# Values in 32-column tiles turned by VectorE, with new planner costs, in a routing-attention and MLP-mixer kernel

## The chip, the core and the metric

The kernel runs on one core of one Trainium2 chip. The metric is the device time of one execution in microseconds (us). Three executions of the kernel before took 811.82 us in the median (810.64 to 812.14).

A core has five engines with queues of their own, each worked off in order: TensorE (matmuls, "PE" in the profile, with its weight loads as "PEld"), VectorE ("DVE"), ScalarE ("ACT"), GpSimd ("POOL") and SyncE ("SP"). SP issues nearly all DMAs here; a few stand in ScalarE's queue. The on-chip memory is one array, `arena`; matmul results land in eight banks of PSUM, `ps`.

## The reference, cut to what is computed

```python
# q, k, v: (4, 8, 768, 64); centroids: (8, 16, 64), all f32
c_n = centroids / (norm(centroids) + 1e-06)                # q_n and k_n likewise
q_assign = argmax(einsum('bhsd,hcd->bhsc', q_n, c_n), -1)  # k_assign likewise
mask = q_assign[:, :, :, None] == k_assign[:, :, None, :]
scores = where(mask, (1 / sqrt(64)) * q @ k^T, -1e9)
attn = softmax(scores) @ v                                 # per batch and head
x = attn.transpose(0, 2, 1, 3).reshape(4, 768, 512)
h = relu(x^T @ w_tok1) @ w_tok2                            # (512, 768) by (768, 256) by (256, 768)
u = x + h^T
out = u + relu(u @ w_ch1) @ w_ch2                          # (768, 512) by (512, 1536) by (1536, 512)
```

The weights of the mixer come as 8-byte words, and the kernel rebuilds f32 values from their two halves with integer work on VectorE (`weight_round`).

## The kernel before, in words

**Recording and planning.** The kernel doesn't emit instructions directly. Helpers (`mm`, `copy`, `halves`, `tt`, `vec`, `dma`, `transpose`) record operations in a `Program`, each with the engines that may run it, a cost in us, and the parts of memory that it reads and writes. `Program.run` plans: matmuls keep the order in which they were recorded; on every other engine, an operation is chosen among those that are ready in the plan, by its due time. The plan is made with `COST`, `LAT` and the costs written at the calls, and the instructions are then emitted in the planned order. Since a helper records everything, nearly all matmuls have line L829, all two-input adds L868, ScalarE's and VectorE's plain copies L848 and L850, copies of 16-bit halves L858, DMA issues L888 and DMA transposes L893.

**Attention.** There are 4 batches x 8 heads; two heads form a pair, so 16 pairs `m`, one after the other. The 768 tokens of a pair are 6 tiles of 128, or two halves of 384. Per pair TensorE does, in this order:

- `scores`: 12 chunks (two halves `u` of the queries by six key tiles `i`). In each chunk, two f32 matmuls of 64 rows, one for each head, and two bf16 matmuls that add the mask out of one-hot cluster codes `M`. ScalarE takes the exp of 768 columns of each chunk (L1122) out of one of three pairs of PSUM banks.
- `values`: 24 matmuls of 64 columns by 384, two heads beside each other, into banks 6 and 7; the result has head dimension by token. ScalarE copies it to `avs`.
- `route` for pair `m + 2`: four matmuls of 32 columns by 384 give the cluster scores. On VectorE: a transpose of 32x32 blocks out of PSUM (L1044), a maximum (L1045), a comparison, a transpose back (L1049). On ScalarE: the one-hot codes `rb` with a count of hits (L1053). `rb` then goes through DRAM into `M`; for pair 0 through eight small DMAs inside `arena`.
- `sums`: VectorE adds up the exps over key tiles (three adds for each half, two of 1536 and one of 768 columns), four matmuls with a matrix of ones give the softmax denominators, which are copied to `denS`.
- `finish_x`: six transposes of `avs` and three of `denS` on TensorE; on VectorE the reciprocal, and two multiplications out of PSUM that write `x`.

For pairs 0 to 2 the queries and keys are turned by TensorE (`turn_qk`). From pair 3 on `dma_turn_qk` does it: ScalarE takes the 16-bit halves apart (four copies of 768 columns), two DMA transposes turn them, and ScalarE joins them in two copies of 1536 columns. Meanwhile VectorE prepares the mixer's weights in 31 pieces of up to 512 columns, together with the sums that the seven-product scheme below needs, and stores them in DRAM (`wdt`, `wd1`, `wd2`).

**Mixer.** All four products of the mixer are done as seven half-size products in place of eight (`token1`, `token2`, `product`), with sums and differences on VectorE and GpSimd. `channel1` and `channel2` run over two groups of two batches. In them GpSimd does differences of operands (`tsum`) and sums of products (`combine`) on 384 or on 3 x 384 columns, VectorE drains PSUM with adds (L868) and does the other sums, ScalarE the relu (L875). Out of the same weights ScalarE computes range sums (L1759), and `check` (L1771 to L1804) compares counts at the end, in the middle of the last group's work; a general path stands behind a flag and isn't taken here.

**Before the first scores.** The centroids are loaded and normed on VectorE, turned on TensorE and copied into `cbd`; pair 0 is loaded by two queues (keys by SP, queries by ScalarE's), turned, routed; pair 1 is turned while the codes of pair 0 are made; three chunks of scores without mask are done ahead, then `route(1)`, then the masks.

## Time and profile before

| What | us |
|---|---|
| Profiled execution, its own time | 812.03 |
| its span | 810.2 |
| Median of three executions | 811.82 |
| Start of the first masked scores | 19.13 |
| First weight load of pair 1's scores | 41.26 |
| First matmul of the mixer | 345.03 |
| Last matmul | 804.8 |

How to read the lines: times are in us from the start of the span unless marked ns. A group line gives line, engine, operation, output and input shapes (partitions x elements) and count, then busy time and the mean ns of one, then the idle time of the engine just before them and what ended it. A timeline line gives start, duration, engine, line and operation; equal neighbours are merged with their count, and the bracket tells how long the engine was idle before, and who released it. A line of the windows view gives a stretch, its length, the busy time and count of each engine, the granted TensorE clock, the share of busy DMA engines, and GB/s. An f32 matmul is recorded as two, each with its own weight load. The ends of matmuls are modelled, so the spacing of weight loads tells more about TensorE's pace than its busy time does.

### The profile page before, as it was taken

The numbers are of one execution on the slowest core, as the hardware profiler recorded it, in microseconds if no ns is written. First come the engines' busy times: TensorE is split into PE (matmuls) and PEld (weight loads), VectorE is DVE, ScalarE is ACT, GpSimd is POOL, SyncE is SP. The second block draws the span as 40 slices with busy tenths as digits, with TensorE's granted clock in tenths as the row PEclk, the third lists the DMA queues.
The fourth block names the chain that finished last, engine by engine and source line by source line (L and its number), as shares of the span: only waits on it lengthen the run. The fifth ranks groups of instructions, "written<-read, shape, count | busy, mean of one in ns | idle before, by whom it ended". The sixth has DMA issues, their size and how long they took to land.

```text
span 810.2 us, 10859 instructions
## 1 busy us (share of the span) xinstructions
PE 791.3 (98%) x3743; PEld 429.2 (53%) x3743; DVE 678.1 (84%) x873; ACT 473.0 (58%) x612; POOL 178.8 (22%) x124
## 2 busy tenths in 40 slices
PE   5999999999999999999999999999999999999997
PEld 3444445554444445444555555555555555555554
DVE  3789999999999999998898867699975686789984
ACT  3688888888888875699913236433464504400424
POOL 1000000000000000000345398500196379620000
PEclk9999999999999999999999999999999999999999
DMA  5777778879888984369739765556899833333766
GB/s 123 213 181 179 179 195 207 211 181 226 204 210 182 226 236 115 82 132 222 146 85 260 202 199 177 184 176 202 239 252 239 223 109 107 97 96 99 160 156 167
DMA packets 265120, 143.49 MB, mean 177 GB/s; under 512 B 184289, under 2 KB 260961, under 8 KB 265057
## 3 DMA queue, kind: packets, MB, share of 16 engines
q1 hardware_dynamic: 262560, 141.88, 68.7%
q10 hardware_dynamic: 2496, 0.84, 0.4%
q8 instruction: 32, 0.52, 0.3%
q14 instruction: 32, 0.25, 0.1%
HBM read 91.95 MB, written 28.61 MB: 149 GB/s over the span
## 4 chain that ended last, share of the span: by engine, by line
PE 95%; DVE 1%; issue 1%; DMA 0%; ACT 0%; SPq 0%; ACTq 0%
PE ps L829 95%; DVE arena L868 0%; DVE arena L850 0%; DMA arena<-arena 0%; ACT arena L1122 0%; ACT arena L848 0%; SPq L888 0%; DVE arena L1244 0%; DVE arena L1045 0%; DVE arena L1044 0%; ACT arena L1053 0%; DVE arena L1790 0%; ACTq L848 0%
## 5 line engine op out<-in xcount | busy, mean ns | idle before, releaser
L829 PE MATMUL ps<-arena 128*128 128x384 f32 (+6 forms) x3743 | 791.3, 464 | 13.5 <-DVE arena L981 5.7
L829 PEld LDWEIGHTS ps<-arena 128*128 128x128 f32 (+3 forms) x3359 | 409.8, 169 | 349.3 <-issue 143.4
L868 DVE TENSOR_TENSOR arena<-arena 128x1536 f32<-128x1536 f32 (+6 forms) x355 | 369.0, 1064 | 14.8 <-ACT arena L1122 7.3
L868 POOL TENSOR_TENSOR arena<-arena 128x384 f32<-128x384 f32 (+1 forms) x116 | 175.4, 1538 | 534.3 <-DVE arena L868 396.7
L868 DVE TENSOR_TENSOR arena<-ps,arena 128x384 f32<-128x384 f32 (+2 forms) x259 | 207.7, 809 | 79.3 <-PE ps L829 72.0
L858 ACT COPY arena<-arena 128x768 uint16<-128x768 uint16 (+1 forms) x197 | 191.2, 1047 | 45.0 <-DVE arena L868 24.4
L1122 ACT ACTIVATE arena<-ps 128x768 f32<-128x768 f32 x192 | 150.2, 809 | 16.7 <-PE ps L829 13.2
L848 ACT COPY arena<-ps 128x384 f32<-128x384 f32 (+2 forms) x67 | 44.9, 670 | 137.3 <-PE ps L829 127.2
L875 ACT ACTIVATE arena<-arena 128x1152 f32<-128x1152 f32 (+1 forms) x38 | 39.9, 1074 | 56.6 <-DVE arena L868 29.3
L1759 ACT ACTIVATE arena<-arena 128x768 f32<-128x768 f32 x40 | 38.7, 967 | 56.8 <-DMA arena<-in_moe_w_ch_dram 39.9
L829 PEld LDWEIGHTS <-arena 64*128 64x128 bf16 x384 | 19.3, 94 | 26.1 <-issue 1.6
L850 DVE COPY arena<-ps 128x384 f32<-128x384 f32 (+3 forms) x18 | 14.4, 806 | 12.0 <-PE ps L829 10.3
L1044 DVE STREAM_TRANSPOSE arena<-ps 128x384 f32<-128x384 f32 x16 | 9.3, 583 | 15.5 <-PE ps L829 15.5
L1244 DVE SCALAR_TENSOR_TENSOR arena<-arena 128x512 f32<-128x512 uint32 (+1 forms) x31 | 20.7, 691 | 0.2
L1238 DVE SCALAR_TENSOR_TENSOR arena<-arena 128x512 uint32<-128x512 uint32 (+1 forms) x31 | 20.6, 670 | 0.3
L1053 ACT ACTIVATE arena<-arena 128x384 bf16<-128x384 f32 x16 | 11.2, 703 | 10.3 <-DVE arena L1179 10.3
L1241 DVE TENSOR_SCALAR arena<-arena 128x512 uint32<-128x512 uint32 (+1 forms) x31 | 12.7, 429 | 0.2
L1234 DVE TENSOR_SCALAR arena<-arena 128x512 uint32<-128x512 uint32 (+1 forms) x31 | 12.9, 437 | 0.0
L1049 DVE STREAM_TRANSPOSE arena<-arena 128x384 f32<-128x384 f32 x16 | 9.2, 575 | 0.4
L1045 DVE TENSOR_REDUCE arena<-arena 128x24 f32<-128x384 f32 x16 | 8.8, 553 | 0.6
L1759 ACT ACTIVATION_READ_ACCUMULATOR arena<-arena 128x1 f32 x40 | 7.5, 189 | 0.0
L1186 DVE RECIPROCAL arena<-arena 128x12 f32<-128x12 f32 x16 | 3.6, 228 | 0.5
(47 smaller groups left out, 21.4 us busy)
## 6 DMA issues: line engine op xcount, KB each, us to landing
arena<-wd SPq DMA_DIRECT2D x196, 192.0 KB, 2.4
wd<-arena SPq DMA_DIRECT2D x84, 224.0 KB, 3.9
arena<-in_moe_w_ch_dram SPq DMA_DIRECT2D x48, 256.0 KB, 4.5
arena<-in_moe_w_ch_dram SPq DMA_DIRECT2D x16, 768.0 KB, 4.4
arena<-in_v_dram SPq DMA_DIRECT2D x16, 384.0 KB, 4.4
out_dram<-arena SPq DMA_DIRECT2D x14, 384.0 KB, 3.7
arena<-in_k_dram SPq DMA_DIRECT2D x13, 384.0 KB, 4.3
arena<-in_q_dram SPq DMA_DIRECT2D x13, 384.0 KB, 4.5
```

What stands on the lines that cost most here:

```text
L829: nc.tensor.matmul(dst, lhsT=lhsT, rhs=rhs, start=start, stop=stop, tile_position=pos, is_transpose=tr, skip_group_check=True,)
L848: nc.scalar.copy(out=dst, in_=src)
L850: nc.vector.tensor_copy(out=dst, in_=src)
L858: nc.scalar.copy(out=dst, in_=src)
L868: (nc.vector if e == "DVE" else nc.gpsimd).tensor_tensor(out=dst, in0=a, in1=b, op=op)
L875: nc.scalar.activation(out=dst, in_=src, func=ACT.Relu)
L1122: lambda e, ex=ex, s=s: nc.scalar.activation(out=ex.ap, in_=ps[:, 2 * s : 2 * s + 2, 0:HS], func=ACT.Exp, scale=SM_SCALE),
L1234: vec(lambda: nc.vector.tensor_scalar(out=hh, in0=hi, scalar1=0x07FFFFFF, scalar2=3, op0=ALU.bitwise_and, op1=ALU.logical_shift_left,), f, ...
L1238: vec(lambda: nc.vector.scalar_tensor_tensor(out=TT, in0=hi, scalar=0xC0000000, in1=hh, op0=ALU.bitwise_and, op1=ALU.bitwise_or), 0.14 + 0 ...
L1241: vec(lambda: nc.vector.tensor_scalar(out=hh, in0=TT, scalar1=0xFF800000, scalar2=None, op0=ALU.bitwise_and), f, T.k(), h.k())
L1244: vec(lambda: nc.vector.scalar_tensor_tensor(out=ll, in0=lo, scalar=float(2.0**-52), in1=hh.bitcast(F32), op0=ALU.mult, op1=ALU.mult,), 0. ...
L1759: lambda e, i=i, func=func, bias=bias, n=n, hi=hi: nc.scalar.activation(out=hi, in_=hi, func=func, bias=bias, accum_out=wsum.ap[:, i, n : ...
```

## The change

In the attention, a pair is one function. The scores go by key tile, with both halves of the queries in a row. Values are done in tiles of 32 columns by 192 tokens: for each key tile sixteen matmuls, four column groups (32 tokens of each 128) by two heads by two halves of the head dimension. Their result has 32 x 32 blocks that VectorE turns straight from PSUM into `x`, and then scales in place; the denominators are done in the same way. TensorE's nine transposes, `avs` and `denS` go. `sums` has eight matmuls in place of four, `es` has one add less for each half. `route(m + 2)` stands before the fifth key tile of values, `sums` before the sixth.

`dma_turn_qk` is split: `part_qk` may start after the exps of the current pair, `join_qk` likewise, and the join is four copies of 768 columns instead of two of 1536.

At the start, both queues load keys first, sixteen matmuls of the identity by itself (`keep_busy`) stand around the centroids' turn, three chunks of scores stand ahead of pair 1's turn and route, and the codes of pair 0 go into a mask of their own (`M0`) by eight copies or scalings on ScalarE or VectorE instead of eight DMAs.

The planner gets other costs, a price for a change of the tile shape on TensorE, and start times for the weight pieces of 14 us and 13 us more for each. GpSimd's adds over 3 x 384 columns become three of 384.

```diff
 COST = {
-    "ACT": (0.17, 0.00083),
-    "ACT16": (-0.1, 0.00128),
-    "DVE": (0.16, 0.00104),
+    "ACT": (0.09, 0.00083),
+    "ACT16": (-0.36, 0.001426),
+    "DVE": (0.075, 0.00104),
...
+SWITCH = 0.1
+SELF = 0.13
+START, STEP = 14, 13
...
-    LAT = {"PE": 0.2, "ACT": 0.15, "DVE": 0.12, "POOL": 0.15, "SP": 0.0}
+    LAT = {"PE": 0.2, "ACT": 0.22, "DVE": 0.2, "POOL": 0.15, "SP": 0.0}
...
-                    t = max(free[e], o.ready)
+                    t = max(free[e] + (SWITCH if o.mode != mode else 0.0), o.ready)
...
-        for i, a, qu in ((1, k, queues[0]), (0, q, queues[1])):
-            for h in range(2):
+        for i, a in ((1, k), (0, q)):
+            for h, qu in enumerate(queues):
...
-        for M in Ms:
-            g.add({"POOL": 1.0}, lambda e, M=M: nc.gpsimd.memset(M.ap, 0.0), [], M.k())
+        vec(lambda: nc.vector.memset(M0.ap, 0.0), 0.5, [], M0.k())
+        keep_busy(11)
...
         turn(ps[:, 7, 0:P], sq.ap[:, 0:P], sq.k(), bank(7))
+        keep_busy(5)
...
+    def keep_busy(n):
+        for _ in range(n):
+            mm(ps[:, 5, 0:P], ident.ap, ident.ap, True, True, 0.22, ident.k(), bank(5))
...
-    def dma_turn_qk(m):
+    def part_qk(m):
         for n in range(2):
...
-                halves(h.ap[:, :, :, hd], src[:, :, hd, :, :, n], S, qkr.k(), h.k())
+                halves(
+                    h.ap[:, :, :, hd], src[:, :, hd, :, :, n], S,
+                    qkr.k() + [("exps", m - 3)], h.k(),
+                )
...
+    def join_qk(m):
...
         for n in range(2):
-            halves(dst[:, :, :, n], qkt[n].ap, 2 * S, qkt[n].k(), T.k())
+            for r in range(0, NQK, NJ):
+                halves(
+                    dst[:, r : r + NJ, :, n], qkt[n].ap[:, r : r + NJ], S,
+                    qkt[n].k() + [("exps", m - 2)], T.rows(r, r + NJ),
+                )
...
-            for gr in range(4):
+            for gr in (0, 2, 3, 1):
                 i, u = divmod(gr, 2)
                 for h in range(2):
-                    dma(
-                        M.ap[64 * h : 64 * h + C, i, u * HS : (u + 1) * HS],
-                        rb.ap[32 * gr + C * h : 32 * gr + C * h + C], rb.k() + M.k(),
-                        [("mask", m % 2, i, u, h)], 12, 768, 0.0, ("SP", "ACT")[h],
+                    rows = slice(32 * gr, 32 * gr + 32)
+                    dst = M0.ap[64 * h : 64 * h + 32, i, u * HS : (u + 1) * HS]
...
+                    g.add(
+                        {"ACT": (0.5, 0.65)[i], "DVE": (0.35, 0.45)[i]}, place0,
+                        o.k() + msc0.k() + M0.k(), [("mask", 0, i, u, h)],
                     )
...
+        def chunk(n):
+            return divmod(n, NJ) if m == 0 else divmod(n, 2)[::-1]
...
         if m == 0:
+            turn_qk(1, (7, 6, 7))
+            load_qkr(3, 26.0)
             route(1, 6)
...
-            tt(a.ap, x.ap, y.ap, ALU.add, 4 * HS, x.k() + y.k(), a.k())
-            tt(a.ap, a.ap, z.ap, ALU.add, 4 * HS, a.k() + z.k(), a.k())
-            tt(a.ap[:, 0], a.ap[:, 0], a.ap[:, 1], ALU.add, 2 * HS, a.k(), a.rows(0, 1))
+            tt(a.ap, x.ap, y.ap, ALU.add, 2 * S, x.k() + y.k(), a.k())
+            tt(a.ap, a.ap, z.ap, ALU.add, 2 * S, a.k() + z.k(), a.k())
...
+    def tokens(ap, gr):
+        return ap.rearrange("p (j t) -> p j t", t=P)[:, :, 32 * gr : 32 * gr + 32]
...
+    def values(m, i):
+        V, ex = vs[m % 3], unit[m][i]
+        mms(
+            [
+                (
+                    ps[32 * gr : 32 * gr + 32, 6 + h, c * HS // 2 : (c + 1) * HS // 2],
+                    V.ap[:, h, i, 32 * c : 32 * c + 32], tokens(ex.ap[:, h], gr),
+                    i == 0 and c == 0, i == NJ - 1, (0, 32 * gr),
+                )
+                for h in range(2) for c in range(2) for gr in range(4)
+            ],
+            1.29, V.k() + ex.k(), bank(6, 7), (P, 32),
+        )
...
-        for u in range(2):
-            for j in range(HJ):
-                turn(
-                    ps[:, banks[u], j * P : (j + 1) * P], avs.ap[:, u, j * P : (j + 1) * P],
...
+        vec(lambda: nc.vector.transpose(out=denT.ap, in_=ps[:, bk, 0:HS]), 0.57, bank(bk), denT.k())
...
+        vec(
+            lambda: nc.vector.transpose(
+                out=x.ap[:, :, cols].rearrange("p j (c d) -> p c j d", d=32),
+                in_=ps[:, 6:8, 0:HS],
+            ),
+            0.96, bank(6, 7), xk,
+        )
+        xv = x.ap[:, :, cols].rearrange("p j (h d) -> p j h d", h=2)
+        tt(
+            xv, xv,
+            rcp.ap.rearrange("p h j -> p j h").unsqueeze(3).to_broadcast([P, NJ, 2, D]),
+            ALU.mult, S, xk + rcp.k(), xk,
+        )
...
+    def pair(m):
+        scores(m)
+        if m >= 1 and m + 2 < NP:
+            join_qk(m + 2)
+        if m:
+            next_qk(m)
+        for i in range(NJ):
+            if i == 4 and 1 <= m < NP - 2:
+                route(m + 2, 0)
+            if i == NJ - 1:
+                sums(m, 5)
+            values(m, i)
+        finish_x(m, 5)
...
+        after = START + STEP * npiece
...
-                tt(d, x, y, op, n * HS, xk + yk, dk, engines)
+                w = 1 if engines == ("POOL",) else n
+                for r in range(0, n, w):
+                    tt(
+                        d[:, r : r + w], x[:, r : r + w], y[:, r : r + w], op, w * HS,
...
-            tt(ts[i].ap, a[0], b[0], ALU.subtract, half * HS, a[1] + b[1], ts[i].k(), sums)
+            n = 1 if sums == ("POOL",) else half
+            for r in range(0, half, n):
...
-        scores(m)
-        values(m)
...
+        pair(m)
```

228 lines of the change are left out of this document (126 added, 102 removed).

## The prediction

> **What bounds the kernel now.** I read the page first (busy table, chain of waits), then the windows view with the boundaries of the attention pairs, then the timeline of TensorE's weight loads, because the page's matmul ends are modelled and a matmul that waits looks busy there.
>
> ```profile
> span 810.2 us, 10859 instructions
> PE 791.3 (98%) x3743; PEld 429.2 (53%) x3743; DVE 678.1 (84%) x873; ACT 473.0 (58%) x612; POOL 178.8 (22%) x124
> PE 95%; DVE 1%; issue 1%; DMA 0%; ACT 0%; SPq 0%; ACTq 0%
> ```
> ```profile
> 0.00:41.26 41.26, 31.14 (x198) 16.86 (x198) 23.39 (x54) 20.49 (x31) 3.34 (x8) 1.00 0.64 171
> 41.26:306.54 265.28, 265.28 (x1887) 131.90 (x1886) 243.51 (x354) 227.18 (x282) 0.00 (x0) 1.00 0.82 201
> 306.54:326.47 19.93, 19.77 (x139) 9.90 (x138) 19.27 (x26) 11.39 (x16) 0.00 (x0) 1.00 0.36 88
> 326.47:345.03 18.56, 18.56 (x129) 8.93 (x128) 17.72 (x20) 13.38 (x17) 0.00 (x0) 1.00 0.42 96
> 345.03:810.20 465.17, 456.58 (x1399) 261.56 (x1395) 374.19 (x422) 200.51 (x267) 175.41 (x116) 1.00 0.65 171
> ```
> The columns are the stretch, its length, then busy time with counts of PE, PEld, DVE, ACT and POOL, granted clock, DMA share, GB/s. The rows are: the start with pair 0; pairs 1 to 13 (265.28 / 13 = 20.41 us each); pair 14; pair 15; the mixer. TensorE has no hole in pairs 1 to 13, while DVE is busy 92% and ACT 86%. So TensorE's own work sets the time of a pair, and I price the change by passes of TensorE. One pair, by its weight loads:
>
> ```profile
> 41.26 0.30 PEld L829 LDWEIGHTS ps<-arena 64*128 64x128 f32 x4 [0.17 <-issue]
> 51.15 0.20 PEld L829 LDWEIGHTS ps<-arena 128*64 128x64 f32 x4 [0.48 <-DVE arena L1238]
> 51.53 0.14 PEld L829 LDWEIGHTS ps<-arena 128*64 128x64 f32 x2 [0.18 <-issue]
> 58.30 0.14 PEld L829 LDWEIGHTS ps<-arena 128*64 128x64 f32 x2 [0.18 <-issue]
> 59.04 0.16 PEld L829 LDWEIGHTS ps<-arena 128*32 128x32 f32 x8 [0.60 <-ACT arena L858]
> 59.39 0.13 PEld L829 LDWEIGHTS ps<-arena 128*32 128x32 f32 x4 [0.19 <-issue]
> 59.72 0.13 PEld L829 LDWEIGHTS ps<-arena 128*32 128x32 f32 x4 [0.19 <-issue]
> 60.47 0.98 PEld L829 LDWEIGHTS ps<-arena 128*128 128x128 f32 x9 [0.62 <-ACT arena L848]
> 61.62 0.30 PEld L829 LDWEIGHTS ps<-arena 64*128 64x128 f32 x4 [0.17 <-issue]
> ```
> The reader sees four blocks: scores 9.89 us (41.26 to 51.15), values 7.89, route and sums 1.43, nine transposes 1.15. An f32 matmul is recorded as two passes. From 51.53 to 58.30 lie 21 steps, so a pass over 384 columns takes 0.3224 us, whether two tiles of 64 columns run in it or, at 59.04 to 59.72, four of 32. The 24 passes of values are 7.74 of their 7.89; the other 0.15 goes into entering and leaving the tile shape. A transposing pass over 128 columns takes 0.98 / 9 = 0.109. On the line through these two points a pass over 192 columns takes 0.109 + (64 / 256) x 0.2134 = 0.1624.
>
> **The change part by part.** The sum goes against the profiled run's 812.03 us, 1.83 outside its span and 0.21 above the median shown.
>
> *Values in 32-column tiles, turned by VectorE.* Removed per pair: nine TensorE transposes with their two changes of shape, ScalarE's copy of the values, a copy of the sums. Values become 96 matmuls of 32 columns by 192 tokens instead of 24 of 64 by 384: 48 half passes, 48 x 0.1624 = 7.80 (exact halves would be 7.74). Sums double to 4 x 0.3224 = 1.29, route stays 2 x 0.3224 = 0.645, and all three share one tile shape, so 0.15 is paid once. The block is 9.88, the pair 9.89 + 9.88 = 19.77, a gain of 0.64. Pairs 1 to 13 give 8.3. Pair 14, without route, goes from 19.93 to 19.12: 0.8. Pair 15 goes from 18.56 to 19.12, a loss of 0.56, but its transposes (0.98) leave the mixer: 0.4. Pair 0 like the others: 0.6. Together **10.1 us**.
>
> The cover of VectorE's and ScalarE's new work is TensorE's 19.77 us per pair. The rows by shape:
>
> ```profile
> L868 DVE TENSOR_TENSOR arena<-arena 128x1536 f32<-128x1536 f32 x80 | 140.7, 1763 | 11.2 <-ACT arena L1122 7.3 <-ACT arena L848 0.6
> L868 DVE TENSOR_TENSOR arena<-arena 128x768 f32<-128x768 f32 x40 | 39.6, 992 | 1.2
> L868 DVE TENSOR_TENSOR arena<-ps,arena 128x384 f32<-128x384 f32 x170 | 92.4, 553 | 29.2 <-PE ps L829 22.2 <-ACT arena L858 0.2
> L1044 DVE STREAM_TRANSPOSE arena<-ps 128x384 f32<-128x384 f32 x16 | 9.3, 583 | 15.5 <-PE ps L829 15.5
> L858 ACT COPY arena<-arena 128x768 uint16<-128x768 uint16 x171 | 142.8, 912 | 45.0 <-DVE arena L868 24.4 <-DMA arena<-arena 16.5 <-PE ps L829 3.1
> L1122 ACT ACTIVATE arena<-ps 128x768 f32<-128x768 f32 x192 | 150.2, 809 | 16.7 <-PE ps L829 13.2 <-issue 2.1 <-ACT arena L1122 0.7
> L868 POOL TENSOR_TENSOR arena<-arena 128x384 f32<-128x384 f32 x84 | 90.0, 1090 | 513.5 <-DVE arena L868 394.2 <-PE ps L829 116.0 <-DMA wd<-arena 2.9
> L868 POOL TENSOR_TENSOR arena<-arena 128x1152 f32<-128x1152 f32 x32 | 86.3, 2713 | 20.8 <-PE ps L829 14.2 <-DVE arena L868 2.6 <-DVE arena L1786 2.3
> ```
> VectorE loses 4 x 1.76 + 2 x 0.99 of adds and 2 x 0.55 of scaling (10.1) and gets 4 x 1.76 of adds, a transpose of 384 (0.58), one of 768 (twice 0.58 at most) and a scaling of 768 (0.99): 9.8. So it is no fuller than its 92%. ScalarE loses the values' copy and swaps two wide copies for four of 768. Both are priced at nothing; a rival has what that costs if the cover fails.
>
> *ScalarE's copies between scores phases.* In one queue now stand: twelve exps, eight copies, the one-hot of route, the next exps. Counted from the pair's first load, the scores end at 9.9, the last exp (0.81) at 10.9 with 0.2 for the wait, which is an estimate, and eight copies of 0.91 at 18.2. Route starts behind four tiles of values, at 9.89 + 0.15 + 4 x 1.30 = 15.2, and ends at 15.9; its VectorE chain takes 2.4 (12.36 to 14.74 in the rows below) and a wait: 18.5. The one-hot (0.71 + 0.19 below) ends at 19.4, and the next exp is wanted at 19.77 + 0.81 + 0.2 = 20.8. The slack is 1.4 us: price nothing.
>
> *Start: keys first, fillers, mask by copies.*
>
> ```profile
> 1.01 0.29 POOL masks.py:199 TENSOR_SCALAR_AFFINE_SELECT arena<-arena 128x128 f32<-128x128 f32 x1
> 7.13 2.80 PE L829 MATMUL ps<-arena 128*128 128x128 f32 x12 [0.94 <-DMA arena<-in_k_dram]
> 12.36 0.58 DVE L1044 STREAM_TRANSPOSE arena<-ps 128x384 f32<-128x384 f32 x1 [1.71 <-PE ps L829]
> 14.16 0.58 DVE L1049 STREAM_TRANSPOSE arena<-arena 128x384 f32<-128x384 f32 x1
> 15.66 0.71 ACT L1053 ACTIVATE arena<-arena 128x384 bf16<-128x384 f32 x1
> 16.27 0.19 ACT L1053 ACTIVATION_READ_ACCUMULATOR arena<-arena 128x1 f32 x1
> 16.54 2.82 ACTq L888 DMA_DIRECT2D arena<-arena  x4
> 17.36 0.16 PEld L829 LDWEIGHTS ps<-arena 128*32 128x32 f32 x8 [0.55 <-issue]
> 19.13 0.81 PE L829 MATMUL ps<-arena 64*128 64x384 bf16 x6 [0.92 <-DMA arena<-arena]
> ```
> Masked scores start at 19.13, after eight small DMAs (from 16.54), by each of the two queues four. The DMAs go; eight copies or scalings of 32x384 take their place, of which the first chunk needs four, two on each engine: about 1 us by the 0.55 row, instead of 2.6. But route of pair 1 stands ahead of the first mask on TensorE; it starts at 17.36 and runs until about 18.2. If the first passes stay as slow as now (2.80 / 12 = 0.23 against 0.109), 0.9 is won. If the sixteen filler matmuls bring the full rate earlier, 24 transposes fall from about 5.6 to 2.6 and route by 0.6: up to 4.5. If the fillers are slow themselves, 32 passes x 0.23 = 7.4 from 1.3 on (the identity's end) push the key transposes from 7.13 past 8.5: a loss of 1.4. I take **2.3**, between the first two ends, because the late copies on ScalarE eat some. [...] The rows show only that the rate is halved at 7.13.
>
> *GpSimd in rows.* The mixer's holes in TensorE:
>
> ```profile
> 657.40 2.49 DVE L1790 TENSOR_SCALAR arena<-arena 128x20 f32<-128x20 f32 x1
> 661.20 1.24 PE L829 MATMUL ps<-arena 128*128 128x384 f32 x3 [1.25 <-DVE arena L868]
> 707.51 3.71 DVE L868 TENSOR_TENSOR arena<-arena 128x1152 f32<-128x1152 f32 x1
> 711.79 1.53 PE L829 MATMUL ps<-arena 128*128 128x384 f32 x4 [1.59 <-issue]
> ```
> A VectorE op on 20 elements takes 2.49 us, an add of 1152 takes 3.71, both while GpSimd runs adds of 1152 (2.71 each); the PSUM drains behind them come late, and TensorE waits 1.25 and 1.59. In rows a GpSimd add takes 1.09, so each wait shrinks by about 1.6 at most and the holes nearly close. GpSimd itself gets 32 x (3 x 1.09 - 2.71) = 18 us more, hidden in its idle 78%; without that cover a late operand would open new holes of the same size. Bounds -2 to +2.8; I take **2.0**.
>
> *Scheduler costs and weight pieces every 13 us.* These move work among engines that are not the bound. The order of TensorE's mixer matmuls stays. Nothing.
>
> The sum: 812.0 - 10.1 - 2.3 - 2.0 = **797.6 us**.
>
> **The rivals.**
>
> *A: the tiles are bound by issue, and the kernel gets slower.* Each half pass needs four loads and four matmuls in 0.162 us. The densest stretch in the rows is 59.04 to 60.47, sixteen loads and sixteen matmuls in four passes: one pair of instructions per 0.081. If that is the limit, a half pass costs 0.322, and 16 x 48 x 0.16 = 123 us are added: 920. It turns the sign once a half pass exceeds 0.162 + 14.4 / 768 = 0.181. For it: no row shows twice that density. Against: within 59.04 eight loads take 0.16 us, so the instructions themselves follow much faster than the passes, and the pass, not the issue, sets the 0.322. [...] Chance 0.12.
>
> *B: VectorE's route chain is late, and ScalarE's queue stops the exps.* Behind the one-hot stand twelve exps, and behind them TensorE's scores. It decides from 1.4 us of lateness; an add of 1.76 and one of 0.99 ahead of the chain make 2.75, so 1.35 x 13 = 17.5 us are given back: 815.1. For it: VectorE at 92%. Against: TensorE never waits in 265 us now, with longer ScalarE copies between exps. Chance 0.08.
>
> *C: the side edits do not do what they say.* Fillers in the way (+1.4) and new GpSimd waits (+2): 812.0 - 10.1 + 3.4 = 805.3. Chance 0.10.
>
> **How the numbers follow.** The forecast, 797.6, has 0.70; its own range is 794 to 802, from the start's and the mixer's bounds. A, B and C have 0.12, 0.08, 0.10. The range 792.5 to 808 holds the forecast's range, C, and the milder half of B (an add of 1.76 alone: 802). A measurement tells 0.2% (1.6 us) from no change. Faster: 0.70 + 0.10 and a little of A and B, 0.82. Same: 0.03, out of the same two. Slower: the rest of A and B, 0.15.
>
> **What would show it.** Right: a windows row with pairs of 19.7 to 19.8 us; loads of 128x32 in fours every 0.16 us; first masks before 18 us; no DVE op on 20 elements over 1.3 us. Wrong: fours every 0.18 or more (A); TensorE waiting on an ACT exp once per pair (B); key transposes after 8.5 us, or holes in the mixer released by POOL (C).

## The result and the profile after

The changed kernel takes 803.11 us in the median of four runs (802.45 to 803.79). Four runs of the kernel before beside them have a median of 811.98: three lie at 810.64 to 812.14, and a slow one of 1197.51 us is left out of the ratio. The ratio is 0.9891, with a 95% interval from 0.9878 to 0.9904. That is faster, as forecast, and inside the wide range of 792.5 to 808, but outside the 794 to 802 that the forecast gave itself, and 5.5 us above its 797.6: of a gain of 14.4 us, 8.9 came. The profiled execution took 803.35.

The page of the changed kernel, its span, busy table and chain of waits:

```profile
span 801.3 us, 15484 instructions
PE 785.5 (98%) x6063; PEld 467.3 (58%) x6063; DVE 663.9 (83%) x863; ACT 468.0 (58%) x615; POOL 189.6 (24%) x185
PE 83%; DVE 10%; ACT 4%; issue 2%; POOL 0%; DVEq 0%; POOLq 0%; ACTq 0%
```

TensorE is as busy as before, but the chain of work that ends last now runs through VectorE and ScalarE for 14% of its way, against 1% before. So other engines have come within reach of being the bound. Where, the windows view of the changed kernel tells; its boundaries answer to those of before (start with pair 0; pairs 1 to 13; pair 14; pair 15; mixer):

```profile
0.00:38.38 38.38, 32.92 (x373) 22.50 (x373) 28.72 (x69) 19.89 (x32) 0.70 (x6) 1.00 0.67 178
38.38:295.45 257.07, 257.07 (x3745) 160.43 (x3745) 229.87 (x317) 220.27 (x286) 0.00 (x0) 1.00 0.80 192
295.45:314.56 19.11, 19.11 (x284) 12.08 (x280) 18.59 (x24) 9.69 (x12) 0.00 (x0) 1.00 0.62 151
314.56:333.68 19.12, 19.12 (x284) 12.08 (x280) 18.74 (x24) 12.56 (x16) 0.00 (x0) 1.00 0.42 100
333.68:801.30 467.62, 457.24 (x1390) 260.21 (x1386) 367.95 (x433) 205.60 (x271) 188.88 (x179) 1.00 0.68 177
```

| Stretch | before, us | after, us | difference | forecast |
|---|---|---|---|---|
| start and pair 0 | 41.26 | 38.38 | -2.88 | -2.9 |
| pairs 1 to 13 | 265.28 | 257.07 | -8.21 | -8.3 |
| pair 14 | 19.93 | 19.11 | -0.82 | -0.8 |
| pair 15 | 18.56 | 19.12 | +0.56 | +0.56 |
| mixer to the end of the span | 465.17 | 467.62 | +2.45 | -3.0 |

A pair takes 257.07 / 13 = 19.77 us. Every row up to the mixer came out as forecast, the first one by luck: the masked scores start 2.95 us earlier, not 2.3, but from there to pair 1 it is 22.20 us after (38.38 - 16.18) and 22.13 before, so that the 0.6 us forecast for pair 0 didn't come. The whole miss of 5.4 us is in the last row. Three cuts take it apart. The first is at the end of the mixer's token stage, about 86 us after its start:

```profile
333.68:420.00 86.32, 84.58 (x230) 41.94 (x226) 83.08 (x148) 61.39 (x77) 17.64 (x17) 1.00 0.86 182
420.00:695.18 275.18, 275.12 (x853) 161.43 (x853) 202.41 (x194) 118.25 (x162) 161.67 (x157) 1.00 0.67 192
```

and the same view of the kernel before, cut as long after its own mixer began:

```profile
345.03:431.40 86.37, 86.31 (x246) 44.47 (x243) 76.67 (x130) 61.61 (x79) 18.93 (x19) 1.00 0.72 154
431.40:705.90 274.50, 273.25 (x847) 160.00 (x845) 212.04 (x198) 112.88 (x156) 148.76 (x96) 1.00 0.67 190
```

In the token stage of before TensorE had no hole (86.31 of 86.37), though it still did the nine transposes of the last pair (0.98). After, it stands still for 1.74 us (86.32 - 84.58), while VectorE is busy 83.08 of 86.32, 6.4 us more than before. Since matmul ends are modelled, the windows hide a part: by the spacing of TensorE's weight loads there are eight holes of 0.2 to 0.75 us, 3.1 us in all, against one of 0.2 before. From there to the first of the three-column matmuls of `check` (695.18 after, 705.90 before) the holes went from 1.25 us to 0.06. Together the two rows take 361.50 us after and 360.87 before. The second cut is at the last VectorE copy, the third at the end of the span. The chain view ends, in the changed kernel, in

```profile
793.43 0.56 DVE arena L862
```

and in the kernel before in

```profile
804.87 0.56 DVE arena L850
```

From the three-column matmuls to the end of that copy it is 98.81 us after (793.99 - 695.18) and 99.53 before. So the mixer up to its last copy is 0.09 us shorter, where 2.98 was forecast (2.0 of holes, 0.98 of transposes).

From the copy's end to the end of the span lie 801.3 - 793.99 = 7.3 us after, and 810.2 - 805.43 = 4.8 before: 2.5 us more for the same closing work.

### The profile page after: what moved, and what is told of

The parts are those of the page before. It is cut to its first block, busy times and chain, and to the rows that moved or that the text cites. A ratio compares the mean times of both kernels' runs of the same rounds, so it can differ in the third digit from the quotient of the medians.

```text
span 801.3 us, 15484 instructions
## 1 busy us (share of the span) xinstructions
PE 785.5 (98%) x6063; PEld 467.3 (58%) x6063; DVE 663.9 (83%) x863; ACT 468.0 (58%) x615; POOL 189.6 (24%) x185
## 4 chain that ended last, share of the span: by engine, by line
PE 83%; DVE 10%; ACT 4%; issue 2%; POOL 0%; DVEq 0%; POOLq 0%; ACTq 0%
PE ps L841 68%; PE ps L1207 15%; DVE arena L880 7%; ACT arena L870 2%; ACT arena L1190 1%; DVE arena L1330 1%; DVE arena L1333 0%; DVE arena L1263 0%; DVE arena L1336 0%; ACT arena L860 0%; ACT arena L887 0%; DVE arena L1326 0%; DVE arena L1249 0%; DVE arena L862 0%; DVE arena L1085 0%
## 5 line engine op out<-in xcount | busy, mean ns | idle before, releaser
L841 PE MATMUL ps<-arena 128*128 128x384 f32 (+5 forms) x2735 | 641.3, 462 | 7.9 <-DVE arena L862 2.1
L841 PEld LDWEIGHTS ps<-arena 128*128 128x128 f32 (+1 forms) x2351 | 341.5, 185 | 252.8 <-issue 58.6
L880 DVE TENSOR_TENSOR arena<-arena 128x256 f32<-128x256 f32 (+6 forms) x340 | 354.1, 1062 | 22.9 <-ACT arena L1190 14.2
L880 POOL TENSOR_TENSOR arena<-arena 128x384 f32<-128x384 f32 x179 | 188.9, 1085 | 514.8 <-DVE arena L880 390.9
L880 DVE TENSOR_TENSOR arena<-ps,arena 128x384 f32<-128x384 f32 (+3 forms) x227 | 189.1, 843 | 88.7 <-PE ps L841 85.2
L870 ACT COPY arena<-arena 128x768 uint16<-128x768 uint16 x223 | 191.4, 948 | 47.9 <-DMA arena<-arena 22.3
L1207 PE MATMUL ps<-arena 128*32 128x192 f32 (+1 forms) x3328 | 151.1, 339 | 0.0
L1207 PEld LDWEIGHTS ps<-arena 128*32 128x32 f32 x3328 | 106.5, 110 | 48.0 <-issue 20.3
L860 ACT COPY arena<-ps 128x1152 f32<-128x1152 f32 (+2 forms) x42 | 30.8, 738 | 105.4 <-PE ps L841 105.4
L1263 DVE STREAM_TRANSPOSE arena<-ps 128x768 f32<-128x768 f32 x16 | 15.6, 975 | 1.1 <-PE ps L1207 1.0
L1249 DVE STREAM_TRANSPOSE arena<-ps 128x384 f32<-128x384 f32 x16 | 9.2, 577 | 3.0 <-PE ps L1207 2.9
```

The lines of the kernel that those rows point to most:

```text
L841: nc.tensor.matmul(dst, lhsT=lhsT, rhs=rhs, start=start, stop=stop, tile_position=pos, is_transpose=tr, skip_group_check=True,)
L860: nc.scalar.copy(out=dst, in_=src)
L870: nc.scalar.copy(out=dst, in_=src)
L880: (nc.vector if e == "DVE" else nc.gpsimd).tensor_tensor(out=dst, in0=a, in1=b, op=op)
L1207: nc.tensor.matmul(dst, lhsT=lhsT, rhs=rhs, start=start, stop=stop, tile_position=pos, skip_group_check=True,)
L1263: lambda: nc.vector.transpose(out=x.ap[:, :, cols].rearrange("p j (c d) -> p c j d", d=32), in_=ps[:, 6:8, 0:HS],),
```

## The experiments

All runs below are the changed kernel with the edits shown; their ratios are to the kernel before, whose median was 812.0 to 812.1 beside each of them.

**SyncE's code shifted.** In the changed kernel's trace, SyncE does nothing for 2.31 us (797.89 to 800.20) between two of its closing semaphore instructions, though the output had landed at 797.0. The edit adds a second DMA issue for each of the 31 weight pieces to SyncE's code in the general path, which isn't taken, so that all code behind it moves and nothing that runs is changed.

```diff
-        nc.sync.dma_start(raw[:, 0:n].rearrange("p n two -> p (n two)"), src.bitcast(U32))
+        for _ in range(2):
+            nc.sync.dma_start(raw[:, 0:n].rearrange("p n two -> p (n two)"), src.bitcast(U32))
```

> The changed kernel with more SyncE instructions in the path behind the flag, which is not taken; nothing that runs is changed, only where SyncE's last instructions lie in its code. Theory (the 2.3 us in which SyncE does nothing near the end, 797.89 to 800.20, are a wait for a block of its code): the gap goes, span about 799.0, time about 800.8. Rival (it waits for a late store): the gap stays, 803.1.

Measured: 801.31 us (801.07 to 801.64), ratio 0.9866 (0.9851 to 0.9881). The view of the closing line, with the first and last start of its instructions, in the changed kernel:

```profile
L2000 SPq EVENT_SEMAPHORE  x10: 17/28/28, 797.6 to 801.2; - x10
L2000 POOLq EVENT_SEMAPHORE  x4: 17/17/17, 800.6 to 801.2; - x4
```

and in the shifted one:

```profile
L2001 SPq EVENT_SEMAPHORE  x10: 17/28/28, 797.7 to 798.9; - x10
L2001 POOLq EVENT_SEMAPHORE  x4: 17/17/17, 798.3 to 798.9; - x4
```

Ten instructions of at most 28 ns each are spread over 3.6 us in the one and over 1.2 us in the other, and GpSimd's four begin at 800.6 us in the one and at 798.3 in the other. The profiled spans differ by 2.3 us (801.3 and 799.0), the medians by 1.80. Since only the place of the code differs, the 2.3 us come from that place; I call them the wait for code. What SyncE waits for there, a block of its code as expected or something else, no trace shows. The traces of the other runs agree. In all eleven runs of the changed kernel and its variants whose code isn't shifted, a wait of 1.06 to 2.3 us stands before the 991st instruction that the profile shows of SyncE, whichever of the closing instructions that is. The two with shifted code (this one and the last one below) have none. In the changed kernel it comes thirteen instructions behind the branch over the general path, and no run here tells whether the branch has a part in it.

**No fillers.**

```diff
-        keep_busy(11)
...
-        keep_busy(5)
```

> The sixteen filler matmuls at the start taken out. Theory (they bring TensorE to its full rate before the key transposes): transposes at 0.21 us each again, first masked scores at 17.5 to 18.5 in place of 16.2, time 804.5 to 805.5. Rival (loads and copies set the start): masks at 16.2, time 803.1.

Measured: 805.66 us (803.35 to 806.10), ratio 0.9915 (0.9901 to 0.9928). TensorE's timeline without the fillers: the first block (up to the turn of pair 0), the second (pair 0's route, the scores ahead, most of pair 1's turn) and the one in which the masks begin:

```profile
5.70 3.05 PE L841 MATMUL ps<-arena 128*128 128x128 f32 x13 [5.70 <-DVE arena L992]
9.63 6.32 PE L841 MATMUL ps<-arena 128*32 128x384 f32 x28 [0.88 <-DVE arena L862]
...
17.63 1.45 PE L841 MATMUL ps<-arena 128*32 128x384 f32 x14 [0.68 <-ACT arena L860]
```

and with them, in the changed kernel:

```profile
1.36 7.35 PE L841 MATMUL ps<-arena 128*128 128x128 f32 x45 [1.36 <-POOL arena masks.py:199]
9.58 4.13 PE L841 MATMUL ps<-arena 128*32 128x384 f32 x28 [0.88 <-DVE arena L862]
...
15.39 1.45 PE L841 MATMUL ps<-arena 128*32 128x384 f32 x14 [0.68 <-ACT arena L860]
```

With 13 passes in 3.05 us, 0.23 each, the first turns run at the slow rate of before. With the fillers the passes begin 0.21 us apart and, from 5.8 us on, 4.4 us after the first of them, 0.11 apart. The first block ends at the same time in both, but the second, which takes 6.32 us without them and 4.13 with them, is through 2.2 us earlier. The masked scores start at 18.41 us instead of 16.18 (19.13 in the kernel before). So of the 2.95 us won at the start, 2.2 are the fillers', and 0.7 the copies' and the order's. The other 0.4 us or so of the run's 2.6 are its plan's: its mixer takes 362.1 us up to the three-column matmuls instead of 361.5, pair 15 takes 0.2 us more, and the end of the span 0.8 less.

**GpSimd's adds whole again.**

```diff
-                w = 1 if engines == ("POOL",) else n
+                w = n
...
-            n = 1 if sums == ("POOL",) else half
+            n = half
```

> GpSimd's adds over 3 x 384 columns whole again, all else as changed. Theory (VectorE waits behind long GpSimd adds): one or two holes of 1 to 1.8 us after 600 us come back, with VectorE operations that take over 2 us for little work; time 804.5 to 806. Rival (the new plan avoids them anyway, and rows only cost GpSimd time): 802.5 to 803.3.

Measured: 802.62 us (802.42 to 803.38), ratio 0.9886 (0.9871 to 0.9901): no difference from the changed kernel, and none of the two holes of before comes back. The theory missed, and the rival held. The group rows of VectorE's small operation, which took 2.49 us in the kernel before, show why; here with whole adds:

```profile
L1894 DVE TENSOR_SCALAR arena<-arena 128x20 f32<-128x20 f32 x1 | 0.2, 166 | 0.0
```

It no longer falls beside an add of GpSimd: the planner, with its new durations, put them elsewhere.

**No gate for ScalarE's copies.**

```diff
-                    qkr.k() + [("exps", m - 3)], h.k(),
+                    qkr.k(), h.k(),
...
-                    qkt[n].k() + [("exps", m - 2)], T.rows(r, r + NJ),
+                    qkt[n].k(), T.rows(r, r + NJ),
```

> The planner is no longer told that ScalarE's copies of the scores' halves and of route's tile must stand behind the exps; it places them as it likes. My theory (the order of ScalarE's copies has 1.4 us of slack in every pair, and the attention stretch is set by TensorE at 19.76 us a pair): no change, 802.3 to 804.3, pairs 1 to 13 still 19.75 to 19.80. Rival (the gate keeps the exps' queue clear, rival B of the prediction): pairs grow to 20 us or more, TensorE waits on an exp once in a pair, and the time is 806 or above.

Measured: 810.02 us (809.50 to 810.75, 11 runs), ratio 0.9977 (0.9968 to 0.9986). The rival holds: 6.9 of the 8.9 us that the change won are gone. The mixer starts at 343.23 us, not 333.68, so attention takes 9.55 us more, nearly all of it in pairs 1 to 13; the mixer up to the three-column matmuls takes 2.0 less. ScalarE's timeline in one pair of the changed kernel:

```profile
79.17 9.75 ACT L1190 ACTIVATE arena<-ps 128x768 f32<-128x768 f32 x12 [1.61 <-PE ps L841]
88.82 6.74 ACT L870 COPY arena<-arena 128x768 uint16<-128x768 uint16 x8
96.52 0.71 ACT L1094 ACTIVATE arena<-arena 128x384 bf16<-128x384 f32 x1 [0.96 <-ACT arena L870]
```

and in the same pair without the gate:

```profile
81.99 1.05 ACT L870 COPY arena<-arena 128x768 uint16<-128x768 uint16 x1
82.89 3.66 ACT L1190 ACTIVATE arena<-ps 128x768 f32<-128x768 f32 x5
86.45 1.06 ACT L870 COPY arena<-arena 128x768 uint16<-128x768 uint16 x1
87.36 2.21 ACT L1190 ACTIVATE arena<-ps 128x768 f32<-128x768 f32 x3
```

with TensorE beside it, from the scores of that pair to its first values:

```profile
79.36 8.71 PE L841 MATMUL ps<-arena 64*128 64x384 f32 x60
88.22 1.89 PE L841 MATMUL ps<-arena 64*128 64x384 f32 x12 [0.16 <-ACT arena L1190]
90.04 5.41 PE L1207 MATMUL ps<-arena 128*32 128x192 f32 x128
```

With the gate the twelve exps take 9.75 us in a row beside 9.89 of TensorE's scores, but ScalarE isn't at its limit there: they start (9.75 - 0.81) / 11 = 0.81 us apart, as TensorE delivers. Behind a copy, where scores already wait, five exps take 3.66 us and three 2.21, which is 0.70 to 0.71 apart. So ScalarE has about 12 x (9.89 / 12 - 0.71) = 1.4 us to spare in the scores of a pair; this is an estimate from these rows. A copy holds it for 0.9 us (82.89 - 81.99 and 87.36 - 86.45), and the two together are more than that. TensorE then waits for a pair of PSUM banks, and the scores take 90.04 - 79.36 = 10.68 us. The block of values is unchanged at 9.87.

**The planner's old durations**, in the changed kernel, and then with whole adds too.

```diff
-    "ACT": (0.09, 0.00083),
-    "ACT16": (-0.36, 0.001426),
-    "DVE": (0.075, 0.00104),
+    "ACT": (0.17, 0.00083),
+    "ACT16": (-0.1, 0.00128),
+    "DVE": (0.16, 0.00104),
...
-SWITCH = 0.1
-SELF = 0.13
+SWITCH = 0.0
+SELF = 0.03
...
-    LAT = {"PE": 0.2, "ACT": 0.22, "DVE": 0.2, "POOL": 0.15, "SP": 0.0}
+    LAT = {"PE": 0.2, "ACT": 0.15, "DVE": 0.12, "POOL": 0.15, "SP": 0.0}
```

The costs written at VectorE's small operations, at the exps (0.81, not 0.70) and at the range sums (1.1, not 0.9) go back with them. TensorE's costs stay as changed.

> The changed kernel with the planner's durations, switch and latency of before. My theory (durations move work among VectorE, ScalarE and GpSimd, which cost time only where VectorE is full, and that is the end of attention and the token stage): pairs 1 to 13 within 0.1 us of 19.76, the stretch of 9.9 us blocks unchanged, and the mixer up to its check matmul 361 to 364 us instead of 361.5; 802.5 to 806. Rival (the measured durations are what keeps TensorE fed at 93 per cent load of VectorE): holes of 0.3 to 1 us in most pairs, 808 or above.

> The old planner durations, with GpSimd's adds whole again (three rows of 384 in one instruction). My theory from the run with the old durations alone (rows that follow each other at once on GpSimd kept one add of VectorE on 256 elements waiting 7.6 us; whole adds do the same, since nothing lies between two of them either): the time stays above 815, and rows are no cure and no cause. Rival (it is the rows that make the old durations harmful, for the planner of before, with whole adds and old durations, lost nothing): 808 or below. If it comes out between, the plan decides by chance.

Measured: 827.79 us (825.11 to 830.35), ratio 1.0196 (1.0174 to 1.0218), with rows; 821.39 us (819.22 to 823.36), ratio 1.0118 (1.0093 to 1.0143), with whole adds. Up to the mixer both run as the changed kernel does, save for one block; the loss is in the mixer, which takes 385.1 and 380.2 us up to the three-column matmuls, by the spacing of TensorE's loads, instead of 361.5. The first expectation was half right: the pairs stay, but the loss is eight times the most that I gave it. The second held, for the time stays above 815. The largest hole of the first, in the timeline:

```profile
483.17 11.51 POOL L880 TENSOR_TENSOR arena<-arena 128x384 f32<-128x384 f32 x12
...
486.08 1.36 DVE L880 TENSOR_TENSOR arena<-ps,arena 128x1152 f32<-128x1152 f32 x1 [0.58 <-PE ps L841]
487.35 7.61 DVE L880 TENSOR_TENSOR arena<-arena 128x256 f32<-128x256 f32 x1
...
494.88 2.61 DVE L880 TENSOR_TENSOR arena<-ps,arena 128x1152 f32<-128x1152 f32 x2
...
496.28 1.01 PE L841 MATMUL ps<-arena 128*128 128x384 f32 x1 [6.37 <-DVE arena L880]
```

An add of 256 columns, 0.43 us elsewhere, takes 7.61, to the end of a row of twelve GpSimd adds that follow each other without a gap (483.17 + 11.51 = 494.7). The drain of PSUM stands behind it in VectorE's queue, and TensorE waits 6.37. The add that took 1.36 beside the same GpSimd work has one operand in PSUM, and isn't held up: the 82 adds of its shape take 1.36 in the mean of that run. So here the add with both operands in `arena` waited for eight of GpSimd's rows, and the one with an operand in PSUM didn't. That isn't so everywhere. In the run with 6 us more for a landing, below, an add of the same size has no such wait in the midst of seven rows:

```profile
495.54 7.33 POOL L880 TENSOR_TENSOR arena<-arena 128x384 f32<-128x384 f32 x7
498.22 0.53 DVE L880 TENSOR_TENSOR arena<-arena 128x256 f32<-128x256 f32 x1
```

In the changed kernel, too, VectorE's adds of 768 columns from 585.58 us on come in between rows of GpSimd that follow each other, and take 1.17 to 1.32 us, where the mean of all 24 is 1.01. What decides between the two is open.

So rows are no sure cure. With whole adds the old durations bring back the old picture, in VectorE's timeline of the second run:

```profile
661.54 2.54 DVE L1894 TENSOR_SCALAR arena<-arena 128x20 f32<-128x20 f32 x1
...
715.58 3.71 DVE L880 TENSOR_TENSOR arena<-arena 128x1152 f32<-128x1152 f32 x1
```

which are the 2.49 and 3.71 us of the kernel before; TensorE's holes behind them are 1.56 and 1.59 us in its timeline. In the run with rows these two are gone and the one of 6.37 is there; since the plan is another as well, the rows alone aren't shown to have done it.

**Weight pieces more often: every 10 us.**

```diff
-START, STEP = 14, 13
+START, STEP = 14, 10
```

> Weight pieces may start every 10 us of the plan in place of 13. Theory (weight pieces pushed into the token stage fill VectorE there and open TensorE's holes of about 3 us): fewer than 5 pieces start after the mixer's first matmul (7 now), the stretch from the mixer's first matmul to the 3-column matmul falls from 361.5 to about 359, time 800.1 to 801.6. Rival (VectorE is simply full there, wherever the pieces start): 361.5 and 803.1 stay.

Measured: 806.69 us (806.52 to 807.12), ratio 0.9934 (0.9920 to 0.9947). The mixer did what was expected (359.1 us up to the three-column matmuls instead of 361.5, two pieces instead of seven after its start, 0.7 us of holes in the token stage instead of 3.1), and the total did not: attention took it back. The windows view of this run, cut before the tenth pair and at the end of attention:

```profile
38.40:217.40 179.00, 178.17 (x2592) 111.05 (x2593) 165.18 (x235) 154.75 (x201) 0.00 (x0) 1.00 0.85 204
217.40:341.52 124.12, 120.41 (x1712) 80.01 (x1712) 120.81 (x172) 88.01 (x114) 0.00 (x0) 1.00 0.80 196
```

and the changed kernel from the same pair on:

```profile
216.39:333.68 117.29, 117.29 (x1716) 73.53 (x1712) 112.43 (x154) 87.95 (x112) 0.00 (x0) 1.00 0.79 190
```

VectorE did 8.4 us more in this stretch and TensorE's work took 6.8 us longer. VectorE was at 96% there already (112.43 of 117.29), and most of what is put in comes out at the end.

**Pieces at two rates**, the first seven every 7 us, so that VectorE's idle time in the first pairs is used.

```diff
-        after = START + STEP * npiece
+        after = START + (7 * npiece if npiece < 7 else 49 + 12.5 * (npiece - 7))
```

> The first seven weight pieces are let go every 7 us from 14 us on, the others every 12.5 us, so that all are 46 to 58 us earlier than in the changed kernel. My theory (the pieces that run into the token stage cost it 3 us, the ones in the last third of attention lengthened the pairs when they came every 10 us, and VectorE has room in the first pairs): the token stage's holes go, the mixer up to the check matmul is 358.5 to 359.5 us, the pairs stay at 19.76 to 19.85, time 800.3 to 802. Rival (VectorE at 93 per cent has no room anywhere in attention): pairs in the first third grow as those in the last third did with a piece every 10 us, 0.3 to 1 us each over seven pairs, 804 or above.

Measured: 802.37 us (801.44 to 802.89), ratio 0.9884 (0.9869 to 0.9900), by its interval the same as the changed kernel. The token stage's holes fell from 3.1 to 1.2 us by the spacing of the loads, the mixer up to the three-column matmuls took 360.18 us, and pairs 2 to 14 stayed as they were; but pair 15's scores took 11.42 us instead of 9.89. From the last copy to the end of the span it is 5.67 us, 1.6 less than in the changed kernel: the wait for code is 1.06 here. These 1.6 us are all that the profiled spans differ by (799.6 and 801.3). VectorE's timeline at pair 15:

```profile
315.18 0.42 DVE L1326 TENSOR_SCALAR arena<-arena 128x512 uint32<-128x512 uint32 x1
...
316.82 0.69 DVE L1336 SCALAR_TENSOR_TENSOR arena<-arena 128x512 f32<-128x512 uint32 x1
317.43 0.58 DVE L1249 STREAM_TRANSPOSE arena<-ps 128x384 f32<-128x384 f32 x1
```

The transpose of the denominators out of PSUM (L1249), which frees a bank that the scores use next, stands behind the unpacking of a piece. Neither theory is borne out in full: there is room early, and the same piece of work did harm at another place.

**Pieces less often: every 15 us**, in three steps.

```diff
-START, STEP = 14, 13
+START, STEP = 14, 15
```

> Weight pieces every 15 us instead of every 13, so that about four more of them run after the start of the mixer. My theory (each piece that VectorE unpacks in the token stage delays TensorE there): the token stage loses another 1 to 3 us, pairs stay at 19.76, time 804 to 806. Rival (the token stage's holes are from the adds and not from the pieces): no change, 802.3 to 804.

Measured: 824.27 us (822.27 to 825.13), ratio 1.0150 (1.0133 to 1.0167), 18 us beyond what either theory gave. The token stage didn't lose another us, it won one: 1.9 us of holes by the spacing of the loads, not 3.1. The loss comes later. TensorE's timeline has one hole of 13 us, and VectorE's shows what stands at its end:

```profile
461.22 1.82 DVE L880 TENSOR_TENSOR arena<-arena 128x512 f32<-128x512 f32 x2
470.46 0.43 DVE L1326 TENSOR_SCALAR arena<-arena 128x512 uint32<-128x512 uint32 x1 [7.42 <-DMA arena<-in_moe_w_ch_dram]
...
472.91 1.36 DVE L880 TENSOR_TENSOR arena<-ps,arena 128x1152 f32<-128x1152 f32 x1
```

VectorE is idle for 7.42 us until the last piece's load lands, unpacks it, and only then drains the PSUM tile that TensorE waits for. From 420 to 480 us the granted clock is 0.89 in this run and 1.00 in the changed kernel, and the 13 passes right behind the hole take 6.07 us, 0.47 each instead of 0.32. I read this as a drain put behind a load that the planner thought would land sooner, and had the planner reckon 6 us more for it:

```diff
-                o.lat = bus + LAND - o.end
+                o.lat = bus + LAND + (6.0 if o.mode == "piece" else 0.0) - o.end
...
-            dma(part(raw.ap), src, [], raw.k((2 * c, 2 * (c + w))), w, 512, after)
+            dma(part(raw.ap), src, [], raw.k((2 * c, 2 * (c + w))), w, 512, after).mode = "piece"
```

> The run with pieces every 15 us, but the planner reckons 6 us more from a weight piece's load to its landing, so that it puts other work of VectorE ahead of the unpacking. My theory (the 13.3 us hole of that run is VectorE standing in its own queue at an unpacking whose load had not landed, with the drain of a finished PSUM tile behind it): the hole of 13 us goes, TensorE's holes between 420 and 480 us fall from 19 us to under 6, time 804 to 811. Rival (TensorE needs that weight itself, so it waits wherever the unpacking stands): the hole only moves to a wait on the weight, time 820 or above.

Measured: 829.98 us (828.55 to 831.07), ratio 1.0219 (1.0202 to 1.0236). That theory fell; the hole grew to 19 us. The drain can't be put ahead. Its destination, in `Hs` (from 134 KB of `arena` on), lies over the three buffers in which the pieces land (`raws`, L805, from 134 KB on), so it must wait until the last piece has been read from there. And the last of 31 pieces isn't let go before 14 + 30 x 15 = 464 us. So the next step keeps 15 us but lets none go later than 404, the last start of the changed kernel:

```diff
-        after = START + STEP * npiece
+        after = min(START + STEP * npiece, 404)
```

> Pieces every 15 us, but none let go later than 404 us, which is when the changed kernel lets its last one go; the last five or so come at 404 and not at 419 to 464. My theory, formed after the run with 6 us more for the landing fell (the drain of the mixer's channel stage writes into the words in which a piece's load lands, so it waits until the last pieces are unpacked, and TensorE waits for the drain): without the late start times the hole of 13 us at 474 goes, holes between 420 and 480 us fall from 19 us to under 5, time 803 to 809. Rival (five pieces more in VectorE's queue after 400 us are too many, whenever they are let go): holes of more than 10 us stay, 815 or above.

Measured: 816.39 us (815.53 to 817.36), ratio 1.0056 (1.0039 to 1.0074). The hole of 13 us is gone and the time 7.9 us shorter, so the late start was its cause. But the rest remains, as many holes of 1 to 2 us, and the time is the rival's. The windows view of this run:

```profile
420.00:480.00 60.00, 52.96 (x159) 29.00 (x157) 55.85 (x64) 14.03 (x21) 36.57 (x36) 1.00 0.75 213
```

and of the changed kernel:

```profile
420.00:480.00 60.00, 59.94 (x186) 35.17 (x187) 46.99 (x45) 17.46 (x25) 41.04 (x42) 1.00 0.74 213
```

VectorE at 93% of this stretch, not 78%, and TensorE 7 us of it idle. The start of the last unpacking in the trace, beside the mixer's length (from its start up to the three-column matmuls):

| Run | last unpacking, us | pieces after the mixer's start | mixer, us |
|---|---|---|---|
| every 10 us | 362 | 2 | 359.1 |
| two rates | 367 | 3 | 360.2 |
| no gate | 437 | 7 | 359.5 |
| changed kernel | 427 | 7 | 361.5 |
| every 15, none after 404 | 456 | 10 | 375.3 |
| old durations | 461 | 8 | 385.1 |
| old durations, whole adds | 463 | 8 | 380.2 |
| every 15 us | 470 | 10 | 382.7 |
| every 15, 6 us more to land | 477 | 11 | 390.0 |

In the runs of this table whose last unpacking starts by 437 the mixer's length lies within 2.4 us; where it starts at 456 or later, it is 13.8 us or more beyond the changed kernel, though with the old durations the wait for GpSimd (6.4) is in that. This goes together in nine plans; only for the hole of 13 us has a run shown it to be the cause.

**Three edits together:** shifted code, two rates, 6 us more for a landing.

> Three things together: SyncE's code shifted by 37 instructions, the weight pieces of the first seven every 7 us and the others every 12.5, and 6 us more reckoned for a piece to land. My theory (2.3 us at the end of the span from the code block, 1.3 us of the mixer up to its check matmul, 1.5 us of pair 15 which VectorE's standing at an unpacking cost in the run with two rates): 798.5 to 800. Rival (the savings of the planner's changes do not add, each new plan makes its own holes of 1 to 2 us elsewhere): 801 to 803.

Measured: 802.38 us (801.55 to 803.12), ratio 0.9881 (0.9865 to 0.9898). The rival holds: in this plan pair 15's scores took 11.9 us and pair 1's 11.6. The wait for code is gone once more, with 4.8 us from the last copy to the end of the span. The fastest version is the first one, the shifted code alone, at 801.31.

## Why the prediction was right, and where it was not

*Values in 32-column tiles.* Right, to the size: pairs of 19.77 us and the two last pairs as in the table. The interpolated pass over 192 columns held; the loads of the changed kernel, in the timeline, come in fours:

```profile
48.41 5.03 PEld L1207 LDWEIGHTS ps<-arena 128*32 128x32 f32 x128 [0.48 <-DMA wdt<-arena]
53.48 0.29 PEld L841 LDWEIGHTS ps<-arena 128*32 128x32 f32 x8
```

The first row is 32 fours up to the loads of `sums` behind them: (53.48 - 48.41) / 32 = 0.158 us each, even under the 0.162. Rival A, bound by issue, is dead. No run has the old values in the new kernel; what shows their worth is that the scores stay at 9.89 us and the rest of a pair goes from 10.52 to 9.87, as the sum had it.

*Start.* Right in direction, with 2.3 forecast at the first masks and 2.95 measured. That the 0.65 more is just what pair 0 fell short of is luck. The run without fillers puts the gain on the cause that I had taken only in part: the fillers bring 2.2 of it. The upper bound of 4.5 was not reached; what stands between it and 2.95 was not tried.

*ScalarE's copies.* "Both are priced at nothing" was right for the kernel as it is. But the slack of 1.4 us stood at the wrong place. What decides is not the one-hot's lateness but the exps: by the estimate above they have about 1.4 us to spare in 9.89 (that it is the same figure is chance), two copies of 0.9 are more, and it is the gate that keeps the copies out. Without it attention takes 9.55 us more and the kernel 7. Rival B had the right queue, and the wrong thing in it.

*GpSimd in rows.* The two old holes went, as forecast, but the rows weren't needed for it: with whole adds they are gone as well, and with the old durations and whole adds they are back. The new durations moved the collisions. "In rows a GpSimd add takes 1.09, so each wait shrinks by about 1.6 at most" didn't hold everywhere: with the old durations VectorE waited 7.61 us behind eight rows, though in other places it came in between them.

*Scheduler costs and weight pieces.* This is the step that failed: "These move work among engines that are not the bound ... Nothing." VectorE, at 96% in the last third of attention and in the token stage, is next to the bound there, and moving its work moves the time. With the old durations the same kernel takes 827.79, which is 25 us more. With start times of 14 + 13 n VectorE has 6.4 us more to do in the token stage than before, and the 2.9 us of new holes there (3.1 - 0.2) are the first half of the miss. That the start times move these holes is shown: other start times alone bring them from 3.1 to 0.7 or 1.2 us. How they do it is not shown in full. In the first 86.3 us of the mixer, by the windows view (VectorE busy, TensorE idle) and the spacing of TensorE's loads (worked out for five runs):

| Run | VectorE busy, us | TensorE idle, windows view, us | TensorE's holes by the loads, us |
|---|---|---|---|
| every 10 us | 73.96 | 0.41 | 0.7 |
| two rates | 78.80 | 0.72 | 1.2 |
| no gate | 80.70 | 0.59 | 1.1 |
| every 15 us | 80.99 | 1.13 | 1.9 |
| changed kernel | 83.08 | 1.74 | 3.1 |
| every 15, 6 us more to land | 79.41 | 4.89 | |
| old durations | 76.33 | 2.78 | |
| old durations, whole adds | 74.89 | 2.77 | |

In the first five the holes go with VectorE's load, and not with the number of pieces after the mixer's start. The last three have more idle time at a smaller load, so the load alone doesn't set it; that the order in VectorE's queue does the rest is argued, not shown.

The kernel before, with an order of its own, has 0.2 at 76.67, so some 0.5 to 1 us of the 2.9 may come from another source; that stays open.

*The end of the span.* The sum goes "against the profiled run's 812.03 us" and has no term for the closing work, so it takes it as fixed. It wasn't: there are 2.5 us more at the end, of which 2.3 are SyncE's wait for code, shown by the run that moves nothing but code. No line shown of the profile of before tells it, but a term for it in the range would have been in order.

The miss adds up: 2.9 us of new holes in the token stage and 2.5 at the end of the span are 5.4, against 5.5 between the forecast and the median.

## What to carry to other kernels

Before pricing a planner's or a schedule's change at nothing, look for the engine that is next to the bound in each stage, not over the span: where VectorE was 96% busy, 8.4 us of work moved there cost 6.8, and a start time that is late by tens of us can hold a buffer that something else is to be written into (here 464 us and not 404, which cost 7.9). An in-order queue with about 1.4 us to spare in ten needs its side work gated out, and here the gate was worth as much (9.55 us of attention) as the faster matmuls (8.2 in pairs 1 to 13). A change in the number of instructions moves the code behind it, and here the place of SyncE's last code alone made 2.3 us of span, so a residue of 2 to 3 us at the end of a span is worth one run with nothing but shifted code.

## What the runs showed of the hardware

In one place VectorE's add of two operands in `arena` waited through eight GpSimd adds (7.61 us instead of 0.43); in another the same add took 0.53 in the midst of seven. So cutting GpSimd's work into rows of 384 columns didn't always let VectorE in between. Exps on ScalarE started 0.70 to 0.71 us apart where scores waited for them, though each is shown with 0.81. Matmuls on 32 columns, issued in fours with four weight loads, took 0.158 us a four, which is 0.04 per pair of instructions, half of the densest spacing that the trace of before shows. The first turns of the run without fillers took 0.23 us a pass, where the kernel has 0.109 later; with the fillers the rate changed from 0.21 to 0.11 a pass 4.4 us after the first. Ten closing semaphore instructions of SyncE took 3.6 us or 1.2 us by nothing but the place of their code.
